# An output projection by Strassen's scheme in a routed-attention and gated-FFN kernel

## The chip, the cores and the metric

One core of one Trainium2 chip runs the whole kernel. The metric is device time of one execution in microseconds (us); smaller is better. The engines are TensorE (PE; PEld is its weight load), VectorE (DVE), ScalarE (ACT), GpSimd (POOL) and SyncE (SP, which here only issues DMAs).

## The reference

Batch 4, 8 heads, 768 tokens, head dimension 64, 16 clusters; then an FFN of 512 to 1536 to 512 over 3072 tokens:

```python
q_assign = argmax(einsum('bhsd,hcd->bhsc', q_n, c_n)); k_assign likewise
scores = where(q_assign == k_assign, scale * q @ k.T, -1e9)
attn = softmax(scores)
x = (attn @ v).transpose(0, 2, 1, 3).reshape(B * S, H * D)
gate = 1 / (1 + exp(-(x @ w_gate)))
out = (gate * (x @ w_val)) @ w_out
```

## The kernel before

The program is written out in full, with the order of each engine fixed by hand: a step is one score matmul, and side work hangs on step numbers in the table `SCHED` (`at`, `plan`, `run_bg`). There are 384 steps, 96 for each batch.

**Attention.** A step (`do_scores`) multiplies a key chunk of 128 with 384 queries into a PSUM bank (`sc`, L655), and ScalarE takes the exponential into `es` (L660). Two steps later (`do_av`) three matmuls of 65 columns add to `av` (L678); the 65th column of V's tile `va` is a constant and gives the denominator. After a head, `normalise` (L342 to L347) divides, on VectorE and GpSimd, and a DMA transposes the result into `xT`. Heads of later batches are made ready in the background (`pair_prep`): raw loads on SP, an fp16 high part (VectorE, L1217) and low part (GpSimd, L1218), a DMA transpose into `T` (`turn`, L382), cluster logits (`lg`, L406), the choice of the cluster (L421 to L441), its one-hot rows moved into `T` by SP (`hop`, L462), and `v_cast` and `v_sum` for V (L294, L302 to L309).

**FFN.** Each batch has two blocks of 384 tokens. For each of 12 chunks of the FFN dimension, `gate` runs four matmuls of 384 columns (`g`, L480) and ScalarE a tanh (L488); `val` runs four more (`v`, L500), and VectorE writes `hT = (tanh + 1) * v` in fp16 (L507). Then `outp` multiplies each of the block's three tiles of 128 tokens with `wo`: 12 matmuls of 512 columns into bank `o` (L520), an eviction that scales by 0.5, on ScalarE (L529) or VectorE (L527), and a store on SP (L532). The very last tile is done in three widths (`closing`, L552 to L562). These pieces, with a cost in ns each, wait in `queue`; after each step `ffn_run(ns)` takes pieces until the budget `ns` of that step is used up. So the FFN of one batch runs between the score matmuls of the next, and the blocks of the last batch run alone at the end.

**PSUM.** Four banks (`ring`) rotate over `sc`, `g`, `v` and `lg`; two hold `av`; two (`op`) hold `o`, and are lent to transposes and V sums (`turns`).

Of the kernel before, what the change touches and what calls it, by code (L numbers as in the profile page):

```python
# [8 lines left out]
FP = mybir.dt.float32  # L9
# [89 lines left out]
def kernel(  # L99
# [44 lines left out]
    tp = pool("T", 10)  # L144
    tbp = pool("TB", 4)
# [9 lines left out]
    osp = pool("os", 3)  # L155
    smp = pool("sm", 3)
# [6 lines left out]

    def turns(n=768, dt=HP, name="turns"):
        return op.tile([128, n], dt, tag="o", name=name)


    WB = SCHED.get("wb", 0)
    warm = const.tile([128, 128 if WB else 512], HP, name="warm")
# [13 lines left out]
    def raw(side):  # L183
        return rawp.tile([128, 2, NCH, 64], FP, tag=f"{side}raw", name=f"{side}raw", bufs=SCHED.get(f"{side}rb", 4))
# [8 lines left out]
    def load(eng, side, b, p):  # L193
        t = RAW[side, b, p] = raw(side)
        eng.dma_start(out=t, in_=view(side, b, p))
# [6 lines left out]
    def load_chunks(eng, side, p, part):  # L202
        if part == 0:
            RAW[side, 0, p] = raw(side)
        c = slice(Q0, NCH) if part else slice(0, Q0)
        eng.dma_start(out=RAW[side, 0, p][:, :, c], in_=view(side, 0, p)[:, :, c])

    def load_half(eng, side, part):
        if (side, 0, 0) not in RAW:
            RAW[side, 0, 0] = raw(side)  # L210
        c = slice(0, Q0) if side == "q" else slice(KC, NCH) if part else slice(0, KC)
        eng.dma_start(out=RAW[side, 0, 0][:, 0, c], in_=view(side, 0, 0)[:, 0, c])
# [17 lines left out]
    WOP = SCHED.get("wop", 2)  # L230
    WON = NFC // WOP
    wo = [wpool.tile([128, WON, DM], HP, name=f"wo{i}") for i in range(WOP)]
# [15 lines left out]


# [34 lines left out]
    vas = [const.tile([128, 2, NCH, 65], HP, name=f"va{i}") for i in range(6)]  # L284
    for t in vas:
        DVE.memset(t[:, :, :, 64:65], 1.0)
    for t in vss:
        DVE.memset(t[:, :, 64:65], float(NCH))
# [178 lines left out]
    def ffn_atoms(xT, t0, n, b, ch, final=False):  # L467
        hT = htp.tile([128, NFC, 384], HP, name="hT")
        gv, outs = [], []
        OA = SCHED.get(f"oa{b}{t0}", SCHED.get("oa", 4))  # L470
        cost = NDC * max(n, 80) / 2.4 + 3

        def gate(fc, st, part):
            def f():
                need(("w", fc // WQ, 0), *(("x", b, p, t0 // 128 + c) for p in range(NP) for c in range(n // 128)))
                if part == 0:
                    st.append(bank(512, name="g"))
                g = st[0]
                for dc in range(GA * part, GA * part + GA):
                    PE.matmul(  # L480
                        out=g[:, 0:n], lhsT=wg[fc // WQ][:, dc, fc % WQ, :],
                        rhs=xT[:, dc, t0 : t0 + n],
                        start=(dc == 0), stop=(dc == NDC - 1),
                    )
                if part < NDC // GA - 1:
                    return
# [6 lines left out]
        def val(fc, st, part):  # L493
            def f():
                need(("w", fc // WQ, 1))
                if part == 0:
                    st.append(bank(512, name="v"))
                w = st[2]
                for dc in range(GA * part, GA * part + GA):
                    PE.matmul(  # L500
                        out=w[:, 0:n], lhsT=wv[fc // WQ][:, dc, fc % WQ, :],
                        rhs=xT[:, dc, t0 : t0 + n],
                        start=(dc == 0), stop=(dc == NDC - 1),
                    )
                if part < NDC // GA - 1:
                    return
                DVE.scalar_tensor_tensor(  # L507
                    hT[:, fc, 0:n], st[1][:, 0:n], 1.0, w[:, 0:n], ALU.add, ALU.mult
                )

            return f

        def outp(t, part, st):
            def f():
                if part == 0:
                    need(*(("wo", i) for i in range(WOP)))
                    st.append(op.tile([128, DM], FP, tag="o", name="o"))
                o = st[0]
                for fc in range(OA * part, OA * part + OA):
                    PE.matmul(  # L520
                        out=o, lhsT=hT[:, fc, bass.ts(t, 128)], rhs=wo[fc // WON][:, fc % WON, :],
                        start=(fc == 0), stop=(fc == NFC - 1),
                    )
                if part == NFC // OA - 1:
                    ob = osp.tile([128, DM], FP, name="ob")
                    if t % 2 or SCHED.get(f"ob{b}{t0}", 0):
                        DVE.tensor_scalar(ob, o, 0.5, None, ALU.mult)  # L527
                    else:
                        ACT.activation(ob, o, AF.Copy, scale=0.5)  # L529

                    def store(ob=ob):
                        SP.dma_start(  # L532
                            out=out[b * S : (b + 1) * S].rearrange("(p c) m -> p c m", c=NCH)[
                                :, ch[t], :
                            ],
                            in_=ob,
                        )

                    d_ = SCHED.get("sd", 0)
                    if d_ > 0 and b < B - 2:  # L540
                        at(step_no[0] + d_, store)
                    else:
                        store()

            return f

        def closing(t, a, z):
            def f():
                w = z - a
                o = bank(w, name="o_end")  # L550
                for fc in range(NFC):
                    PE.matmul(  # L552
                        out=o, lhsT=hT[:, fc, bass.ts(t, 128)],
                        rhs=wo[fc // WON][:, fc % WON, a:z],
                        start=(fc == 0), stop=(fc == NFC - 1),
                    )
                ob = osp.tile([128, w], FP, tag="ob_end", name="ob_end")
                if a:
                    DVE.tensor_scalar(ob, o, 0.5, None, ALU.mult)
                else:  # L560
                    ACT.activation(ob, o, AF.Copy, scale=0.5)
                SP.dma_start(  # L562
                    out=out[b * S : (b + 1) * S].rearrange("(p c) m -> p c m", c=NCH)[
                        :, ch[t], a:z
                    ],
                    in_=ob,
                )

            return f

        for fc in range(NFC):
            st = []
            for i in range(NDC // GA):
                gv.append((cost * GA / NDC, gate(fc, st, i)))
            for i in range(NDC // GA):
                gv.append((cost * GA / NDC, val(fc, st, i)))
        for t in range(n // 128):
            st = []
            if final and t == n // 128 - 1:
                outs.append([(900, closing(t, a, z)) for a, z in SCHED.get("cl", [(0, 256), (256, 384), (384, 512)])])  # L580
            else:
                outs.append([(OA * 216, outp(t, i, st)) for i in range(NFC // OA)])
        return gv, outs

    queue = []
    GA = SCHED.get("ga", 4)

    def ffn_block(*a):
        gv, outs = ffn_atoms(*a)
        for x in gv:  # L590
            queue.append(x)
        for o in outs:
            queue.extend(o)

    def ffn_two(a, b_):
        gv, outs = ffn_atoms(*a)
        gv2, outs2 = ffn_atoms(*b_)
        seq = gv + gv2[0:2]
        for i, o in enumerate(outs):
            seq += o + gv2[2 + 2 * i : 4 + 2 * i]  # L600
        seq += gv2[2 + 2 * len(outs) :]
        for o in outs2:
            seq += o
        queue.extend(seq)

    credit = [0.0]

    def ffn_run(ns):
# [5 lines left out]
        if not queue:  # L614
# [465 lines left out]
    for x in SCHED.get("lo", ["v0", "k1", "q1", "v1", "k2", "q2", "v2", "k3", "q3", "v3"]):  # L1080
        if x == "v0" and SCHED.get("v0h", 0):
            RAW["v", 0, 0] = raw("v")
# [124 lines left out]
    for i in range(WOP):  # L1207
        plan(f"wo{i}", 44 + 6 * i, lambda i=i: load_wo(i))

# [78 lines left out]
    for b in range(B):  # L1288
        xT = xtp.tile([128, NDC, S], HP, tag="xTb", name="xTb")
        key = min(b, 1)  # L1290
        for i in range(2 if b else NPT):
# [5 lines left out]
            for w in range(1 + (cn > 3)):  # L1297
                z = cn // (1 + (cn > 3))
                at(u + lag, lambda xT=xT, b=b, a=c0 + z * w, n=z: ffn_block(
                    xT, 128 * a, 128 * n, b, list(range(a, a + n))))  # L1300
# [18 lines left out]
    ffn_run(1e9)  # L1319
    ffn_block(xT, 384, 384, B - 1, [3, 4, 5], True)  # L1320
# [31 lines left out]
```

## Time and profile before

| | |
|---|---|
| time, median of 3 runs | 326.62 us (326.57 to 326.64) |
| span of the profiled execution, first to last instruction | 326.4 us; its own time is not given apart from the span |
| matmuls of 384 columns: scores, gate, value | 384 each |
| matmuls of 512 columns, output projection | 276, and 36 narrower ones for the last tile |
| scores begin, batch by batch | 8.4, 73.1, 129.7, 206.2 us |
| last score matmul, last matmul | 275.0, 323.0 us |

The span is what the engines' records cover. In the slices a digit is the busy share of an engine in a fortieth of the span, in tenths. In a group's row the first number behind the bar is the busy time of all its instructions in us, the second the mean duration of one in ns.

### The profile page before, as it was taken

The numbers are of one execution on the slowest core, as the hardware profiler recorded it, in microseconds if no ns is written. First come the engines' busy times: TensorE is split into PE (matmuls) and PEld (weight loads), VectorE is DVE, ScalarE is ACT, GpSimd is POOL, SyncE is SP. The second block draws the span as 40 slices with busy tenths as digits, with TensorE's granted clock in tenths as the row PEclk, the third lists the DMA queues.
The fourth block names the chain that finished last, engine by engine and source line by source line (L and its number), as shares of the span: only waits on it lengthen the run. The fifth ranks groups of instructions, "written<-read, shape, count | busy, mean of one in ns | idle before, by whom it ended". The sixth has DMA issues, their size and how long they took to land.

```text
span 326.4 us, 8811 instructions
## 1 busy us (share of the span) xinstructions
PE 318.0 (97%) x3366; PEld 205.8 (63%) x3366; DVE 187.4 (57%) x509; ACT 235.6 (72%) x526; POOL 108.4 (33%) x145
## 2 busy tenths in 40 slices
PE   7899999999999989999999999999999999999996
PEld 4788666766666656666566655666566655654654
DVE  6899567766767766657546655666544322441431
ACT  6788988788899878877677777887778877332420
POOL 6887554054345353324222343323200111000000
PEclk9999999999999999999999999999999999999999
DMA  7999995848977797964795574932731012102002
GB/s 209 358 259 179 263 177 91 207 104 206 242 138 197 138 205 162 257 190 85 124 255 110 169 101 130 238 70 50 141 90 38 2 24 78 44 2 94 6 0 96
DMA packets 77994, 45.14 MB, mean 138 GB/s; under 512 B 56896, under 2 KB 75008, under 8 KB 77952
## 3 DMA queue, kind: packets, MB, share of 16 engines
q1 hardware_dynamic: 73984, 39.73, 50.7%
q0 software_dynamic: 3680, 4.72, 8.7%
q8 instruction: 26, 0.43, 0.5%
q14 instruction: 16, 0.13, 0.1%
q10 hardware_dynamic: 288, 0.13, 0.1%
HBM read 28.34 MB, written 6.29 MB: 106 GB/s over the span
## 4 chain that ended last, share of the span: by engine, by line
PE 86%; DMA 4%; POOL 3%; DVE 3%; issue 2%; SPq 1%; ACT 0%; POOLq 0%
PE g L480 19%; PE v L500 19%; PE o L520 17%; PE sc L655 16%; PE av L678 9%; DMA T<-hl 2%; PE lg L406 2%; DMA kraw<-in_k_dram 2%; PE o_end L552 1%; POOL xp L360 1%; POOL hl L883 1%; POOL hl L1004 1%; PE t_ps L904 0%; PE lg L393 0%; PE t_ps L787 0%
## 5 line engine op out<-in xcount | busy, mean ns | idle before, releaser
L660 ACT ACTIVATE es<-sc 128x384 f16<-128x384 f32 x384 | 175.6, 492 | 42.6 <-PE sc L655 35.6
L655 PE MATMUL sc<-T 128*128 128x384 f16 x384 | 118.0, 325 | 0.7 <-DVE T L985 0.4
L678 PEld LDWEIGHTS <-es 128*128 128x128 f16 x1152 | 81.6, 98 | 49.1 <-ACT es L660 0.2
L678 PE MATMUL av<-va,es 128*128 128x65 f16 x1152 | 97.6, 194 | 0.0
L507 DVE SCALAR_TENSOR_TENSOR hT<-th,v 128x384 f16<-128x384 f32 x96 | 53.1, 554 | 70.3 <-PE av L678 47.4
L500 PE MATMUL v<-xTb,wv 128*128 128x384 f16 x384 | 78.1, 326 | 0.0
L480 PE MATMUL g<-xTb,wg 128*128 128x384 f16 x384 | 78.0, 326 | 0.0
L520 PE MATMUL o<-wo,hT 128*128 128x512 f16 x276 | 75.1, 379 | 0.0
L488 ACT ACTIVATE th<-g 128x384 f32<-128x384 f32 x96 | 47.2, 491 | 25.7 <-DVE hT L507 17.9
L347 POOL TENSOR_TENSOR xp<-t,rec 128x384 f16<-128x384 f32 (+1 forms) x30 | 21.2, 705 | 107.8 <-DVE rec L344 56.4
L480 PEld LDWEIGHTS <-wg 128*128 128x128 f16 x384 | 37.2, 97 | 20.4
L500 PEld LDWEIGHTS <-wv 128*128 128x128 f16 x384 | 37.4, 98 | 19.9
L655 PEld LDWEIGHTS <-T 128*128 128x128 f16 x384 | 37.1, 97 | 1.2 <-DVE T L985 0.7
L520 PEld LDWEIGHTS <-hT 128*128 128x128 f16 x276 | 26.7, 97 | 16.2
L1218 POOL TENSOR_TENSOR hl<-kraw,hl 128x384 f16<-128x384 f32 x22 | 20.4, 925 | 37.5 <-DVE hl L1217 18.2
L342 DVE TENSOR_TENSOR t<-av,sv 128x390 f32<-128x390 f32 (+1 forms) x30 | 14.4, 480 | 20.5 <-PE av L678 16.2
L1218 POOL TENSOR_TENSOR hl<-qraw,hl 128x384 f16<-128x384 f32 x22 | 21.4, 973 | 10.6 <-DVE hl L1217 10.6
L421 DVE TENSOR_REDUCE lgs<-lg 128x192 f32<-128x384 f32 x23 | 12.7, 554 | 13.6 <-PE lg L406 13.6
L529 ACT ACTIVATE ob<-o 128x512 f32<-128x512 f32 x15 | 8.9, 596 | 10.7 <-PE o L520 10.5
L294 POOL CAST va<-vraw 128x768 f16<-128x768 f32 x16 | 13.7, 857 | 2.1 <-DMA vraw<-in_v_dram 2.1
L527 DVE TENSOR_SCALAR ob<-o 128x512 f32<-128x512 f32 x8 | 5.5, 692 | 13.4 <-PE o L520 13.4
L406 PE MATMUL lg<-cm,T 128*128 128x32 f16 x288 | 11.1, 176 | 1.3 <-DMA T<-hl 1.3
(118 smaller groups left out, 239.2 us busy)
## 6 DMA issues: line engine op xcount, KB each, us to landing
vraw<-in_v_dram SPq DMA_DIRECT2D x16, 384.0 KB, 5.9
out_dram<-ob SPq DMA_DIRECT2D x23, 256.0 KB, 2.3
kraw<-in_k_dram SPq DMA_DIRECT2D x15, 384.0 KB, 4.1
qraw<-in_q_dram SPq DMA_DIRECT2D x12, 384.0 KB, 5.0
wg<-in_moe_w_gate_dram POOLq DMA_DIRECT2D x2, 768.0 KB, 9.5
wv<-in_moe_w_val_dram POOLq DMA_DIRECT2D x2, 768.0 KB, 10.5
wo<-in_moe_w_out_dram POOLq DMA_DIRECT2D x2, 768.0 KB, 8.8
qraw<-in_q_dram SPq DMA_DIRECT2D x7, 192.0 KB, 6.9
```

The source lines that it names most:

```text
L342: DVE.tensor_tensor(t[:, 0:nq, :], av, sv, ALU.add)
L347: (eng or POOL).tensor_tensor(x, t[:, 0:nq, 0:64], bcast(rec[:, 0:nq], 64), ALU.mult)
L406: PE.matmul(out=lg[:, bass.ts(i, 32)], lhsT=t[:, c, :], rhs=cm[:, h].rearrange("p s n -> p (s n)"), start=True, stop=True,)
L480: PE.matmul(out=g[:, 0:n], lhsT=wg[fc // WQ][:, dc, fc % WQ, :], rhs=xT[:, dc, t0 : t0 + n], start=(dc == 0), stop=(dc == NDC - 1),)
L488: ACT.activation(th[:, 0:n], g[:, 0:n], AF.Tanh, scale=0.5)
L500: PE.matmul(out=w[:, 0:n], lhsT=wv[fc // WQ][:, dc, fc % WQ, :], rhs=xT[:, dc, t0 : t0 + n], start=(dc == 0), stop=(dc == NDC - 1),)
L507: DVE.scalar_tensor_tensor(hT[:, fc, 0:n], st[1][:, 0:n], 1.0, w[:, 0:n], ALU.add, ALU.mult)
L520: PE.matmul(out=o, lhsT=hT[:, fc, bass.ts(t, 128)], rhs=wo[fc // WON][:, fc % WON, :], start=(fc == 0), stop=(fc == NFC - 1),)
L655: PE.matmul(out=sc.rearrange("p (c t) -> p c t", t=128), lhsT=s["k"], rhs=s["q"], start=True, stop=True,)
L660: ACT.activation(es, sc, AF.Exp, scale=SCALE)
L678: PE.matmul(out=av[:, a0 + s["c0"] + i, :], lhsT=s["es"][:, bass.ts(i, 128)], rhs=VA[b, p][:, e, s["j"], :], start=(first and i == 0 and a ...
L1218: POOL.tensor_tensor(hl[:, :, 64:128], r, hl[:, :, 0:64], ALU.subtract)
```

## The change

For batches b = 1 to 3 the output projection of two tiles of 128 tokens at once is done with seven products instead of eight (the variant of Strassen's scheme with few additions). The FFN dimension is halved (6 chunks each) and so is the output width (256 each). A pair of tiles t1 and t2 plays the two block rows of the left matrix; `wo` and four differences of its parts play the right one. The work falls into these parts:

- *Sums of activations* (`Sums.make`): four fp16 operations of 128x768 per pair on VectorE, put behind given chunks of `val` (`SUMS_AT`); the fourth one behind the product that last reads its input.
- *Differences of weights* (`mix_wo`): four, in two parts each, once, at steps 150 to 204. Three lie in the raw buffers of batch 0's last pair of heads (now `held`), one over a part of `wo`.
- *Products* (`product_out`): seven per group, each of 6 matmuls of 256 columns per pair, alternating between banks x and y; an addition on VectorE (a copy on ScalarE for the first) reads the bank after each product, and two products are added to what the bank already holds.
- *Order*: tiles (0, 1) run as a single pair after block 0, from the list `aside`, every second piece being one of block 1's gate and value pieces. Tiles (3, 2) and (4, 5) run after block 1 as two pairs side by side, in the halves of each bank. While a group is open, `turns` takes a bank of the ring.
- *The factor 0.5* moves into the denominator's constant (2 instead of 1), so the evictions no longer scale, and tanh takes its input as it is.
- *Buffers*: raw tiles 3 per side instead of 4, `T` 8 instead of 10, `va` 5 instead of 6; `wo`'s first row replaces the warm-up tile; output tiles are twice as wide; six `sum` tiles.
- *Budgets* per step for batches 2 and 3 go down by some 4%. The last tile's three widths are gone.

```diff
-    "ns21": 510, "ns22": 500, "ns23": 510, "ns30": 460, "ns31": 460, "ns32": 460, "ns33": 440,
+    "ns21": 491, "ns22": 481, "ns23": 491, "ns30": 443, "ns31": 443, "ns32": 443, "ns33": 423,
-    tp = pool("T", 10)
+    tp = pool("T", 8)
+    sump = pool("sum", 6)
     def turns(n=768, dt=HP, name="turns"):
+        if taken["pair"]:
+            return bank(n, dt, name)
+    def raw(side, b, p):
+        if b == 0 and p == NP - 1:
+            return held[side]
+        return rawp.tile([128, 2, NCH, 64], FP, tag=f"{side}raw", name=f"{side}raw", bufs=3)
+    def mix_wo(i, c):
+        o, a, z = [(T1, B12, B11), (T3, B22, B12), (T2, B22, T1), (T4, B21, T2)][i]
+        c = slice(3 * c, 3 * c + 3)
+        DVE.tensor_tensor(o[:, c], a[:, c], z[:, c], ALU.subtract)
-        DVE.memset(t[:, :, :, 64:65], 1.0)
+        DVE.memset(t[:, :, :, 64:65], 2.0)
-                ACT.activation(th[:, 0:n], g[:, 0:n], AF.Tanh, scale=0.5)
+                ACT.activation(th[:, 0:n], g[:, 0:n], AF.Tanh)
+                for k, x in SUMS_AT[b >= PB, blk].get(fc, []):
+                    sm[x].make(k)
+                if fc == NFC - 1 and pairs and blk == 0:
+                    aside.extend(product_out(b, [sm[(0, 1)]], False))
+    SUMS_AT = {
+        (True, 0): {5: [(3, (0, 1))], 11: [(1, (0, 1)), (2, (0, 1))]},
+        (True, 1): {1: [(1, (3, 2))], 5: [(2, (3, 2)), (3, (3, 2))], 6: [(3, (4, 5))],
+                    11: [(1, (4, 5)), (2, (4, 5))]},
+    }
+        def end1(): ACT.activation(st[C11], st["x"], AF.Copy)
+        def end4(): plus(st[C21], st["y"], st[C11])
+        def end6(): plus(st[C12], st["x"], st[C11])
+        def end5():
+            plus(st[C22], st["y"], st[C11])
+            for m in sums: m.make(4)
+        def end7():
+            plus(st[C21], st["x"], st[C21])
+            plus(st[C22], st["x"], st[C22])
+            for i, m in enumerate(sums): store(st["o2"][:, i], b, m.t2, 1)
+        def end3(): plus(st[C12], st["y"], st[C12])   # stored here at the very end
+        def end2(): plus(st[C11], st["x"], st[C11])   # and stored
+        steps = [
+            ("x", lambda m: tok(b, m.t1, 0), B11, True, end1),
+            ("y", lambda m: tok(b, m.t2, 1), T4, True, end4),
+            ("x", lambda m: m.of[2], T2, True, end6),
+            ("y", lambda m: m.of[1], T1, True, end5),
+            ("x", lambda m: m.of[3], T3, False, end7),
+            ("y", lambda m: m.of[4], B22, False, end3),
+            ("x", lambda m: tok(b, m.t1, 1), B21, True, end2),
+        ]
-        while queue and credit[0] > 0:
-            c, f = queue.pop(0)
+        while (queue or aside) and credit[0] > 0:
+            turn_[0] = 0 if not aside else turn_[0] + 1
+            c, f = (aside if aside and (turn_[0] % 2 == 0 or not queue) else queue).pop(0)
+            plan(f"wt{i}{c}", (150 + 8 * i if i < 3 else 200) + 4 * c, lambda i=i, c=c: mix_wo(i, c))
-    ffn_run(1e9)
-    ffn_block(xT, 384, 384, B - 1, [3, 4, 5], True)
+    ffn_block(xT, 384, 384, B - 1, True)
     ffn_run(1e9)
```

More of the change, by code (lines that the diff above doesn't have):

```diff
@@ L162, in bank, with out_bank @@
         return ring.tile([128, n], dt, tag="ring", name=name)
+    taken = {"op": 0, "pair": False, "last": 1}
+    def out_bank():
+        taken["op"] += 1
+        return op.tile([128, DM], FP, tag="o", name="o")
     def turns(n=768, dt=HP, name="turns"):
+        if taken["pair"]:
+            return bank(n, dt, name)
+        taken["op"] += 1
         return op.tile([128, n], dt, tag="o", name=name)
-    WB = SCHED.get("wb", 0)
-    warm = const.tile([128, 128 if WB else 512], HP, name="warm")
+    WOP = SCHED.get("wop", 2)
+    WON = NFC // WOP
+    wo = [wpool.tile([128, WON, DM], HP, name=f"wo{i}") for i in range(WOP)]
+    WB = 0
+    warm = wo[0][:, 0, :]
     POOL.memset(warm, 0.0)
@@ L464, in hop, with tok, store, f @@
         )
[L467 to L470, printed above, removed]
+    HB = {}
+    def tok(b, t, f):
+        return HB[b, t // 3][:, HF * f : HF * f + HF, bass.ts(t % 3, 128)]
+    def store(src, b, c0, n, m=slice(0, DM)):
+        def f():
+            SP.dma_start(
+                out=out[b * S : (b + 1) * S].rearrange("(p c) m -> p c m", c=NCH)[
+                    :, c0 : c0 + n, m
+                ],
+                in_=src,
+            )
+        d_ = SCHED.get("sd", 0)
+        if d_ > 0 and b < B - 2:
+            at(step_no[0] + d_, f)
+        else:
+            f()
+    def ffn_atoms(xT, t0, n, b, final=False):
+        blk = t0 // 384
+        gv = []
         cost = NDC * max(n, 80) / 2.4 + 3
-        def gate(fc, st, part):
+        pairs = [] if b < PB else [(0, 1)] if blk == 0 else [(3, 2), (4, 5)]
+        sm = {x: Sums(b, *x) for x in pairs}
+        def gate(fc, st):
             def f():
                 need(("w", fc // WQ, 0), *(("x", b, p, t0 // 128 + c) for p in range(NP) for c in range(n // 128)))
[L476 to L479, printed above, removed]
+                if fc == 0:
+                    HB[b, blk] = htp.tile([128, NFC, 384], HP, name="hT")
+                g = bank(512, name="g")
+                for dc in range(NDC):
                     PE.matmul(
@@ L539, in f @@
[L539 to L543, printed above, removed]
-            return f
-        def closing(t, a, z):
-            def f():
-                w = z - a
-                o = bank(w, name="o_end")
-                for fc in range(NFC):
+                    ob = osp.tile([128, 2, DM], FP, name="ob")[:, 0]
+                    if t % 2:
+                        DVE.tensor_copy(ob, o)
+                    else:
+                        ACT.activation(ob, o, AF.Copy)
@@ L583, in ffn_atoms @@
-        return gv, outs
+                        out=st[z][:, e], lhsT=a[:, c, :], rhs=rhs[:, c, :],
+                        start=start and c + e == 0, stop=c == HF - 1, skip_group_check=True,
+                    )
+                if g + G == HF and e == P_ - 1:
+                    end()
+            return f
+        for k in range(7):
+            for e in range(P_):
+                for g in range(0, HF, G):
+                    atoms.append((G * (HD / 2.4 + 2.5), atom(k, e, g)))
+        return atoms
@@ L585 @@
     queue = []
-    GA = SCHED.get("ga", 4)
+    aside = []
     def ffn_block(*a):
[L589 to L604, printed above, removed]
+        queue.extend(ffn_atoms(*a))
```

187 lines of the change are left out of this document (122 added, 65 removed), and 2 rows, old and new, of the table SCHED.

## The prediction

> **What bounds the kernel now.** I read the page first: the share of each engine, the slices, the chain that ended last. Batches are numbered as in the code, b = 0 to 3.
>
> ```profile
> span 326.4 us, 8811 instructions
> PE 318.0 (97%) x3366; PEld 205.8 (63%) x3366; DVE 187.4 (57%) x509; ACT 235.6 (72%) x526; POOL 108.4 (33%) x145
> PE   7899999999999989999999999999999999999996
> DVE  6899567766767766657546655666544322441431
> PEclk9999999999999999999999999999999999999999
> PE 86%; DMA 4%; POOL 3%; DVE 3%; issue 2%; SPq 1%; ACT 0%; POOLq 0%
> ```
>
> The chain is TensorE for 86% of the span, and TensorE is busy in nearly every slice at the full granted clock. Busy time can hide small gaps, so I next took the waits of TensorE alone, and the windows of ten us (columns: length; busy us of PE, PEld, DVE, ACT, POOL with counts; clock; DMA share; GB/s):
>
> ```profile
> PE lg L406 <- DMA T<-hl: 1.3, 1, 1.3
> ...
> 110.00:120.00 10.00, 10.00 (x114) 6.31 (x113) 7.47 (x19) 8.88 (x21) 6.09 (x7) 1.00 0.83 180
> 220.00:230.00 10.00, 10.00 (x103) 6.40 (x102) 7.14 (x18) 7.61 (x18) 4.58 (x5) 1.00 0.33 64
> ```
>
> After the lead-in, one wait stands out: 1.3 us for a transposed tile, near 121 us. Otherwise TensorE never stops, even where VectorE is 71 to 75% busy. So a matmul taken away is worth its full spacing, and a stall put in costs its full length.
>
> **What the change takes from TensorE.** Consecutive matmuls overlap, so the price is not the duration of one but the spacing within a row of the timeline:
>
> ```profile
> 315.26 5.34 PE L520 MATMUL o<-wo,hT 128*128 128x512 f16 x24
> 320.44 1.47 PE L552 MATMUL o_end<-wo,hT 128*128 128x256 f16 x12
> L520 PE MATMUL o<-wo,hT 128*128 128x512 f16 x276 | 75.1, 379 | 0.0
> L552 PE MATMUL o_end<-wo,hT 128*128 128x256 f16 x12 | 1.5, 272 | 0.0
> ```
>
> 512 columns: (5.34 - 0.379) / 23 = 0.2157 us. 256 columns: (1.47 - 0.272) / 11 = 0.1089 us. For b = 1 to 3 there are nine pairs of tiles. A pair took 2 x 12 matmuls of 512 columns; it now takes 7 products x 6 matmuls of 256. 216 x 0.2157 = 46.59 us becomes 378 x 0.1089 = 41.16 us: **-5.43 us**. (The last tile is cut into narrower pieces before; that is under 0.1 us.) The new budgets per step only move matmuls between steps of a full engine, and I cost them at nothing; the cover is the unbroken PE row.
>
> The rows of 256 columns had their 128-column weight loads hidden: twelve loads fit in 1.47 us. The Trainium skill speaks against the change here: "TensorE: Matmul & The Clock Gate", section "Back-to-back issue gap", gives a sustained spacing with weight loads of about 81 ns at 128 columns and 131 ns at 512; a straight line puts 256 at 98 ns, and 378 x 98 - 216 x 131 ns would be an estimated 8.7 us lost. The trace disagrees, with 216 and 109 ns.
>
> **What it adds to VectorE.** Per pair four sums of 128x768 fp16 (36 in all), eight differences of weight parts of the same size (steps 150 to 204), and seven additions per product group from PSUM in place of the 0.5 scalings: 21 of 256 and 21 of 512 elements. Rows for prices (by line, shapes kept apart):
>
> ```profile
> L342 DVE TENSOR_TENSOR t<-av,sv 128x195 f32<-128x195 f32 x12 | 4.3, 359 | 14.3 <-PE av L678 10.6 <-issue 2.0 <-POOL hl L1218 1.7
> L342 DVE TENSOR_TENSOR t<-av,sv 128x390 f32<-128x390 f32 x18 | 10.1, 561 | 6.2 <-PE av L678 5.6 <-POOL hl L1218 0.6
> L917 DVE COPY T<-t_ps 128x768 f16<-128x768 f16 x6 | 3.3, 550 | 0.0
> L883 DVE TENSOR_TENSOR hl<-kraw,hl 128x192 f16<-128x192 f32 x1 | 0.4, 358 | 0.0
> L883 DVE TENSOR_TENSOR hl<-kraw,hl 128x384 f16<-128x384 f32 x1 | 0.5, 548 | 0.0
> L527 DVE TENSOR_SCALAR ob<-o 128x512 f32<-128x512 f32 x8 | 5.5, 692 | 13.4 <-PE o L520 13.4
> L529 ACT ACTIVATE ob<-o 128x512 f32<-128x512 f32 x15 | 8.9, 596 | 10.7 <-PE o L520 10.5
> ```
>
> The L342 rows rise 0.202 us in 195 elements: 0.42 us for 256 elements, 0.69 for 512. No row shows an fp16 sum. Nearest below is the 768-element fp16 copy, 0.55; above, the fp32 pair of L883 carried on to 768, 0.55 + 2 x 0.19 = 0.93. I take 0.55, the same size and type. The Trainium skill ("VectorE: DVE Perf Modes", "What auto-detection actually checks") lets a two-source 16-bit operation reach two elements a cycle, an estimated 0.4 us and a fixed part; no run here shows it yet. Added: 44 x 0.55 + 21 x 0.42 + 21 x 0.69 = 47.5 us, less six scalings of 0.69 and two of 0.29 (4.8): some 43 us. VectorE would be about 70% busy, the level of the two windows above, at which TensorE did not wait. What counts is where single operations stand in front of something.
>
> *The four-bank ring.* Scores, gates and values rotate through four banks:
>
> ```profile
> 253.17 0.81 PE L500 MATMUL v<-xTb,wv 128*128 128x384 f16 x4
> 253.91 0.33 PE L655 MATMUL sc<-T 128*128 128x384 f16 x1
> 254.07 0.81 PE L480 MATMUL g<-xTb,wg 128*128 128x384 f16 x4
> 254.82 0.33 PE L655 MATMUL sc<-T 128*128 128x384 f16 x1
> 254.98 0.81 PE L500 MATMUL v<-xTb,wv 128*128 128x384 f16 x4
> 254.09 0.55 DVE L507 SCALAR_TENSOR_TENSOR hT<-th,v 128x384 f16<-128x384 f32 x1 [0.81 <-PE av L678]
> ```
>
> The bank of the first v is free at 254.64 and wanted by the fourth tile after it at 254.98: 0.34 us of room, and VectorE idle for 0.81 before hT. An operation put ahead of hT is free up to about 1.15 us. Behind a waiting PE stand the next scores, hence the exponentials. In the built order, three places per batch hold two sums, or an addition and a sum, among the logits' operations and v_sum: after chunk 11 of block 0, after chunk 5 of block 1, and behind the fourth product. At 0.55 each, two make 1.1: just hidden. But two SBUF inputs beside GpSimd cost more:
>
> ```profile
> 228.07 1.16 POOL L1218 TENSOR_TENSOR hl<-qraw,hl 128x384 f16<-128x384 f32 x1 [0.86 <-DVE hl L1217]
> 228.50 0.89 DVE L308 TENSOR_TENSOR va<-va 128x128 f32<-128x128 f32 x1
> 248.38 0.28 DVE L308 TENSOR_TENSOR va<-va 128x128 f32<-128x128 f32 x1
> ```
>
> The same operation took 0.89 and 0.28 us. I allow **0.5 us** for both batches (0 to 2.4: six places at 0.4).
>
> *The two product banks, two pairs.* A product is 12 x 0.109 = 1.31 us, and each bank is read before its next product. Inside attention a product spans about 2.1 us with the scores between, and VectorE keeps up, except in b = 1 (whose groups run in b = 2's attention), where the logits' operations stand just before the fourth product's addition; the sixth product then waits some 0.3 us for its sum (0 to 0.8): **0.3**.
>
> In the tail nothing stands between products. From the end of the fourth: signal and addition to 0.8 us, two sums to 1.35 and 1.85 (back to back each adds about 0.5), while the fifth ends at 1.31. The sixth starts 0.1 late. The fifth's bank is read twice, 1.85 to 3.1, and the seventh product, due at 2.7, waits for that: 0.4. Together **0.55 us** (0.3 to 1.35, the upper end with 0.93 per sum).
>
> **The end.**
>
> ```profile
> 323.30 0.29 DVE L559 TENSOR_SCALAR ob_end<-o_end 128x128 f32<-128x128 f32 x1 [0.38 <-PE o_end L552]
> out_dram<-ob SPq DMA_DIRECT2D x23, 256.0 KB, 2.3
> out_dram<-ob_end SPq DMA_DIRECT2D x1, 128.0 KB, 1.7
> out_dram<-ob_end SPq DMA_DIRECT2D x2, 64.0 KB, 1.5
> ```
>
> The last eviction is now 512 elements, 0.69 for 0.29: **+0.4**. The last store is 256 KB instead of 64: 2.3 for 1.5 us to land: **+0.8**. Three more stores of 256 KB are issued in the 2.5 us before it. From 128 to 256 KB the row grows 0.6 us, so four need up to 2.4 us of transfer and the last may queue: **+0.4** (0 to 1.3).
>
> **What is moved on SP.** Three raw buffers per side instead of four (the last pair of batch 0 has its own, in which the weight parts later lie) make loads wait for earlier readers. I compared each load with the last read three pairs back. One is tight:
>
> ```profile
> 112.48 0.83 DVE L1217 CAST hl<-qraw 128x384 f16<-128x384 f32 x1
> 113.03 0.96 POOL L294 CAST va<-vraw 128x768 f16<-128x768 f32 x1
> 113.95 0.91 POOL L1218 TENSOR_TENSOR hl<-qraw,hl 128x384 f16<-128x384 f32 x1
> 113.16 0.47 SPq L195 DMA_DIRECT2D vraw<-in_v_dram  x1
> 114.88 2.46 SPq L382 DMA_TRANSPOSE T<-hl  x1
> 114.88 7.14 DMA T<-hl
> ```
>
> The load of 113.16 now waits for the cast that ends at 113.99. Behind it on SP stand this transpose, the one-hot transpose and the xT transpose. The transpose waits until 114.86 for GpSimd anyway, so that costs nothing. Two weight differences fall before the cast of 112.48, 1.1 us together (1.9 at most), against 0.64 between the cast's end and GpSimd's start and the quarter of this window in which VectorE is idle. The transpose may start 0 to 1.2 us later, and its landing ends the 1.3 us wait found above: **+0.2**. T with 8 buffers and va with 5 are freed many steps before reuse.
>
> **Sum.** -5.43 + 0.5 + 0.3 + 0.55 + 0.4 + 0.8 + 0.4 + 0.2 = -2.28. The profiled span is 326.4; the median of three runs, 326.62, lies 0.2 above it, and I keep that: 326.62 - 2.28 = **324.3 us**.
>
> **Rivals.**
> *Only the columns and the last store count*: all new VectorE work hides, no stall but the last 0.3 of the tail, stores not queued. -5.43 + 0.3 + 0.4 + 0.8 = -3.9, 322.7 us. For it: 43% of VectorE is idle. Against: the bank is read twice before the seventh product.
> *The tail takes it*: sums at 0.93 in the tail (1.35) and the stores fully queued (1.3), the rest as forecast: -5.43 + 1.0 + 1.35 + 1.2 + 1.3 = -0.6, about 326.0.
> *VectorE becomes the bound in attention*: sums at 0.93 and held by GpSimd for 0.6. Two make 2.5 us before an hT against the cover of 1.15 and one product part between (3 x 0.109): about 1.0 us of TensorE at each of six places. 6.0 + 0.8 + 0.2 + 1.35 + 1.6 - 5.43 = +4.5, 331 us; it decides from 0.5 us a place. For it: 0.89 us at 228.50. Against: GpSimd is busy 46% even from 220 to 230 us, so not every sum meets it.
> *Weight loads set the spacing*, so that each of 162 extra matmuls costs a load:
>
> ```profile
> L520 PEld LDWEIGHTS <-hT 128*128 128x128 f16 x276 | 26.7, 97 | 16.2
> ```
>
> 162 x 0.097 = 15.7 on top: about 340 us; the 109 ns spacing speaks against it. The section of the Trainium skill named above is the rule behind it.
>
> **How the numbers follow.** About 0.2%, 0.65 us, is what a measurement can tell from no change. Forecast 0.58 (322.4 to 325.9); only columns 0.10; tail 0.10, of which 0.06 within 0.2%; VectorE bound 0.19; weight loads 0.03. Faster 0.72, same 0.06, slower 0.22. The range runs from the columns alone to the near part of the VectorE case, 322.4 to 327.0, and leaves out the rest of that case and the weight loads.
>
> **What would show it.** Right: 378 matmuls 109 ns apart in the o rows; no wait of PE on hT above a few tenths; a wait of about 0.4 before the last product; 1.6 us more between last matmul and end. Wrong: sums of 0.9 us or more, waits of PE for hT or sum adding up to over 3 us, a spacing above 123 ns (24 x 0.2157 / 42, where the product scheme stops paying), or a longer wait of lg near 121 us.

## The result, and the profile after

| | before | after |
|---|---|---|
| time, median of 4 runs each, same chip | 326.60 us (326.33 to 326.64) | 324.82 us (324.73 to 324.90) |
| ratio to before, 95% interval | | 0.9944 [0.9930, 0.9958] |
| profiled execution: time, span | 326.62, 324.8 us (profile taken again, e1_before) | 324.90, 323.1 us |

The change makes the kernel 1.8 us faster; the forecast was 2.3 us. The kernel before was run and profiled once more beside the experiments. That second profile is the one to compare with: its lines and the page of after are next.

The page of the kernel before, profiled again, its timeline of the cluster logits near 121 us, and its end (columns: start us, us, engine, line, operation):

```profile
span 324.8 us, 8811 instructions
120.50 0.46 PE L406 MATMUL lg<-cm,T 128*128 128x32 f16 x12
318.87 2.81 PE L552 MATMUL o_end<-wo,hT 128*128 128x256 f16 x36
321.72 0.29 DVE L559 TENSOR_SCALAR ob_end<-o_end 128x128 f32<-128x128 f32 x1 [0.38 <-PE o_end L552]
```

The page of the kernel after:

```profile
span 323.1 us, 9150 instructions
PE 314.7 (97%) x3504; PEld 222.1 (69%) x3504; DVE 226.7 (70%) x586; ACT 231.1 (72%) x520; POOL 108.6 (34%) x145
PE   7999999999999999999999999999999999999994
DVE  6899656777667997576879688576867356555654
PEclk9999999999999999999999999999999999999999
PE 87%; DVE 5%; issue 3%; DMA 2%; POOL 1%; SPq 0%; ACT 0%; POOLq 0%; DVEq 0%
```

TensorE still carries the chain. VectorE has 39 us more work and is 70% busy. The row near 120.5 us has no wait in its brackets: the 1.3 us wait for a transposed tile, which the first profile showed, is not there when the same kernel is profiled again.

The waits of TensorE alone, kernel after, from 40 us on (total us, times, longest), and windows of ten us (busy us of PE, PEld, DVE, ACT, POOL; clock; DMA share; GB/s):

```profile
PE sc L788 <- DVE lgs L449: 0.6, 1, 0.6
PE g L529 <- DMA xTb<-xp: 0.5, 1, 0.5
PE o L716 <- DVE sum L632: 0.2, 1, 0.2
PE o L716 <- DVE ob L658: 0.2, 1, 0.2
...
110.00:120.00 10.00, 9.43 (x105) 5.91 (x104) 9.65 (x23) 8.34 (x20) 6.11 (x7) 1.00 0.74 201
190.00:200.00 10.00, 9.79 (x122) 8.11 (x120) 8.17 (x21) 6.16 (x13) 3.14 (x5) 1.00 0.34 74
220.00:230.00 10.00, 10.00 (x110) 6.76 (x108) 8.11 (x21) 7.99 (x19) 3.43 (x4) 1.00 0.51 100
```

The view has four waits, each of them once, and TensorE loses time in the windows in which they lie. At 81% VectorE (220 to 230 us) it loses none; at 97% (110 to 120 us) it loses half a us.

The groups of the kernel after, shapes kept apart (busy us, mean ns of one, idle before):

```profile
L716 PE MATMUL o<-wo,hT 128*128 128x256 f16 x162 | 24.0, 272 | 0.2 <-DVE ob L658 0.2
L626 DVE TENSOR_TENSOR sum<-hT 128x768 f16<-128x768 f16 x9 | 5.9, 650 | 0.2
L632 DVE TENSOR_TENSOR sum<-hT,sum 128x768 f16<-128x768 f16 x9 | 4.7, 550 | 0.0
L276 DVE TENSOR_TENSOR vheld<-wo,wo 128x768 f16<-128x768 f16 x2 | 1.6, 798 | 0.0
L658 DVE TENSOR_TENSOR ob<-o,ob 128x512 f32<-128x512 f32 x21 | 14.1, 688 | 9.6 <-PE o L716 8.9 <-ACT es L793 0.7
L658 DVE TENSOR_TENSOR ob<-o,ob 128x256 f32<-128x256 f32 x21 | 8.4, 414 | 0.1
```

The prices taken for the sums (0.55) and for the additions (0.42 and 0.69) are met where nothing disturbs them. The first sums (650) and the first weight differences (798 here) come out longer.

**Where the 1.71 us of span come from**, from the starts of matmuls, the profile before taken again against the one after. The columns give -5.46, by the count of matmuls and their full-rate spacing. Time lost by spacing is what a matmul starts later than one full-rate spacing behind the one before it; after 40 us it grows from 1.51 to 4.05 us, +2.54. The lead-in before 40 us has +0.32 (it differs by up to 0.7 us among profiles of versions of the kernel after that are alike up to there). From the start of the last matmul to the end of the span it is 4.27 us instead of 3.38, +0.89. The sum is -1.71.

### The profile page after: what moved, and what is told of

The parts are those of the page before. It is cut to its first block, busy times and chain, and to the rows that moved or that the text cites. A ratio compares the mean times of both kernels' runs of the same rounds, so it can differ in the third digit from the quotient of the medians.

```text
span 323.1 us, 9150 instructions
## 1 busy us (share of the span) xinstructions
PE 314.7 (97%) x3504; PEld 222.1 (69%) x3504; DVE 226.7 (70%) x586; ACT 231.1 (72%) x520; POOL 108.6 (34%) x145
## 4 chain that ended last, share of the span: by engine, by line
PE 87%; DVE 5%; issue 3%; DMA 2%; POOL 1%; SPq 0%; ACT 0%; POOLq 0%; DVEq 0%
PE g L529 19%; PE v L545 19%; PE sc L788 17%; PE av L811 10%; PE o L716 10%; PE o L583 4%; PE lg L434 2%; PE oh_ps L1097 1%; PE lg L421 1%; PE t_ps L1037 1%; DMA xTb<-xp 1%; DMA qraw<-in_q_dram 1%; PE wm L879 1%; DVE ob L658 1%; POOL xp L375 1%
## 5 line engine op out<-in xcount | busy, mean ns | idle before, releaser
L658 DVE TENSOR_TENSOR ob<-o,ob 128x256 f32<-128x256 f32 (+1 forms) x42 | 22.6, 551 | 9.7 <-PE o L716 8.9
L716 PEld LDWEIGHTS <-sum 128*128 128x128 f16 x216 | 20.9, 98 | 5.6 <-DVE sum L632 0.7
L716 PE MATMUL o<-wo,hT 128*128 128x256 f16 x162 | 24.0, 272 | 0.2 <-DVE ob L658 0.2
L1354 POOL TENSOR_TENSOR hl<-qraw,hl 128x384 f16<-128x384 f32 x22 | 20.7, 940 | 10.0 <-DVE hl L1353 9.7
L583 PE MATMUL o<-wo,hT 128*128 128x512 f16 x72 | 19.9, 379 | 0.0
L716 PEld LDWEIGHTS <-hT 128*128 128x128 f16 x162 | 15.7, 97 | 4.2 <-issue 0.4
L322 POOL CAST va<-vraw 128x768 f16<-128x768 f32 x15 | 12.9, 860 | 2.5 <-DMA vraw<-in_v_dram 2.5
```

The source lines that it names most:

```text
L583: PE.matmul(out=o, lhsT=HB[b, blk][:, fc, bass.ts(t, 128)], rhs=wo[fc // WON][:, fc % WON, :], start=(fc == 0), stop=(fc == NFC - 1),)
L658: plus = lambda dst, a, z: DVE.tensor_tensor(dst, a, z, ALU.add)
L716: PE.matmul(out=st[z][:, e], lhsT=a[:, c, :], rhs=rhs[:, c, :], start=start and c + e == 0, stop=c == HF - 1, skip_group_check=True,)
L1354: POOL.tensor_tensor(hl[:, :, 64:128], r, hl[:, :, 0:64], ALU.subtract)
```

## The experiments

After the result the theory was: the columns pay as forecast, and what is given back goes to a few single places, where a sum, a weight difference or an addition stands in front of something on VectorE, and to the end. The rivals: the loss is spread out, because VectorE is simply fuller; or part of the gain or loss belongs to the other edits (budgets, buffers, the factor 0.5, the undivided last tile), not to the products. e1 to e4 ran on one chip, e5 to e8 on a second, e9 and e10 on a third, each beside the kernel before (326.80, 326.60 and 326.96 us there).

**e1_before: the kernel before, profiled again.** No edit.

> The kernel before, unchanged, to see how its time stands to its span; the changed kernel's time lies 1.8 us above its span. If that offset is common to both, the span here should be near 324.8 us. If the change itself adds something outside the span, the span here stays at 326.4 us and the time at 326.6.

Measured: 326.66 us (326.26 to 327.15), ratio 0.9997 [0.9986, 1.0008]; its profiled execution took 326.62 us with a span of 324.8, and has no wait of `lg`. So the time lies 1.8 us above the span, as in the kernel after (324.90 to 323.1). The first profile, with its span of 326.4, had caught an execution with a wait that is not typical of the kernel: the ten executions of this run have spans of 324.5 to 325.4 us.

**e2_plain: everything but the products.**

```diff
-    PB = 1
+    PB = 4
-    for i in range(4):
-        for c in range(2):
-            plan(f"wt{i}{c}", (150 + 8 * i if i < 3 else 200) + 4 * c, lambda i=i, c=c: mix_wo(i, c))
```

> The changed kernel with the seven products switched off: batches 1 to 3 use the twelve matmuls of 512 columns as batch 0 does, and no weight differences are made; buffers, budgets, the constant 2 and the undivided last tile stay. My theory (TensorE's spacing pays, the other edits cost nothing): span within 0.5 us of the kernel before, time 326.3 to 327.2. Rival (the smaller buffers or budgets give or take time by themselves): over 1 us away. If the 1.5 us outside the span come from these other edits, they show here too.

Measured: 327.54 us (327.16 to 327.83), ratio 1.0021 [1.0011, 1.0031], span 325.6. The other edits together cost 0.9 us, more than the theory allowed and less than the rival asked; the products are worth 2.7 us on top of them (327.54 to 324.82). Of the cost, 0.56 us is the undivided last tile (3.94 us from last matmul start to end, 3.38 before). Two gates lose 0.31 us each; the first, in the timeline of e2:

```profile
186.64 0.19 DVE L372 RECIPROCAL rec<-t 128x6 f32<-128x6 f32 x1
186.85 0.55 DVE L550 SCALAR_TENSOR_TENSOR hT<-th,v 128x384 f16<-128x384 f32 x1
187.46 0.81 PE L529 MATMUL g<-xTb,wg 128*128 128x384 f16 x4
```

The gate's bank is freed by an `hT` that stands behind a head's division. No sum is near: a place in the ring is lost here by the order of the steps alone. Which of the other edits moved it was not taken apart.

**e3_mixlate: the weight differences from step 193 on.** In the kernel after, the first ones lie near 113 us (DVE, POOL and PE in the timeline of after):

```profile
113.12 1.07 DVE L276 TENSOR_TENSOR vheld<-wo,wo 128x768 f16<-128x768 f16 x1
114.11 0.97 DVE L1353 CAST hl<-qraw 128x384 f16<-128x384 f32 x1
115.01 0.54 DVE L449 TENSOR_REDUCE lgs<-lg 128x192 f32<-128x384 f32 x1
112.86 0.91 POOL L1354 TENSOR_TENSOR hl<-kraw,hl 128x384 f16<-128x384 f32 x1 [0.35 <-POOL xp L375]
115.61 0.32 PE L788 MATMUL sc<-T 128*128 128x384 f16 x1 [0.57 <-DVE lgs L449]
```

The difference starts while GpSimd's operation of 112.86 runs, and ends 0.4 us after that one's end at 113.77: it takes 1.07 us instead of the 0.55 that the same shape takes when undisturbed. The Trainium skill ("SBUF — State Buffer", "Who interferes with whom") states that a VectorE instruction with two SBUF inputs is blocked by a GpSimd instruction that reads SBUF and was issued first, until that one is finished; the trace agrees. The cast and the reading of the logits' bank follow it on VectorE, and the next scores want that bank: 0.74 us of TensorE, counted by spacing.

```diff
-            plan(f"wt{i}{c}", (150 + 8 * i if i < 3 else 200) + 4 * c, lambda i=i, c=c: mix_wo(i, c))
+            plan(f"wt{i}{c}", 193 + 7 * i + 3.5 * c, lambda i=i, c=c: mix_wo(i, c))
```

> The eight weight differences are moved from steps 150 to 204 to steps 193 to 218, all else as in the changed kernel. My theory: the wait of 0.7 us of a score matmul on the logits near 115 us goes, and the wait of 1.5 us for the transposed tile near 122 us, which the kernel before has and the changed one lacks, comes back in part, because the order on SP moves back: between -0.7 and +0.8 us. Rival (the differences merely load VectorE): about 0.7 us faster.

Measured: 323.51 us (323.32 to 325.19), ratio 0.9913 [0.9885, 0.9940], span 321.8. The 0.74 us is gone; the wait for `xTb` falls from 0.62 to 0.11; spacing losses after 40 us fall from 4.05 to 3.10. Another 0.40 us is a shorter lead-in, which the edit does not touch. So the span is 1.4 us shorter, more than theory and rival had, and not all of it is the edit's. The wait for `xTb` changes from execution to execution: e6 and e8, the same program up to there, have 0.22 and 0.44. One of the four executions took 325.19 us, so the interval meets that of the kernel after. A wait near 121 us did not come back.

**e4_sum6: the fourth sum behind another addition.** The sums made in `end5` stand in front of the sixth product (0.38 us by spacing in attention, 0.10 in the tail).

```diff
+        def end6(): plus(st[C12], st["x"], st[C11])
+            for m in sums: m.make(4)
         def end5():
             plus(st[C22], st["y"], st[C11])
-            for m in sums: m.make(4)
```

> The fourth sum of each pair is made one product earlier, behind the addition of the third product instead of the fourth. My theory: the waits before the sixth and seventh products of two pairs side by side go (0.38 us near 196 us, 0.10 and 0.34 us near 316 us): 0.5 to 0.9 us faster than the changed kernel. Rival (VectorE as a whole is too loaded, so the wait only moves): within 0.3 us of it.

Measured: 324.65 us (324.54 to 324.82), ratio 0.9936 [0.9922, 0.9951], 0.17 us from the kernel after. The timeline of e4 (DVE, PE):

```profile
195.47 1.88 DVE L658 TENSOR_TENSOR ob<-o,ob 128x512 f32<-128x512 f32 x3
196.20 0.49 PE L716 MATMUL o<-wo,sum 128*128 128x256 f16 x3 [0.62 <-DVE ob L658]
```

In attention the wait changed its name and grew, from 0.38 on the sum to 0.78 on the additions queued behind the logits' operations. In the tail, with no logits, the two waits of 0.10 and 0.34 became one of 0.23. The rival, that the wait only moves, holds in attention; the theory holds in the tail.

**e5_budget: e3 with the budgets of before.**

```diff
-    "ns20": 500, "ns21": 491, "ns22": 481, "ns23": 491, "ns30": 443, "ns31": 443, "ns32": 443, "ns33": 423,
+    "ns20": 520, "ns21": 510, "ns22": 500, "ns23": 510, "ns30": 460, "ns31": 460, "ns32": 460, "ns33": 440,
```

> On the kernel with the later weight differences: the budgets per step of batches 2 and 3 back at the values of the kernel before. In the kernel without products two gates waited 0.31 us each for a bank whose VectorE reader stood behind a head's division. My theory (the lower budgets moved the values onto the divisions; what is left is worth a few tenths): 0.3 us faster to 0.3 us slower. Rival (the lower budgets are needed because the products are shorter): over 0.5 us slower.

Measured: 326.50 us (324.42 to 327.23), ratio 0.9975 [0.9953, 0.9997], span 324.7: nearly the whole gain is gone, as the rival had it. The timeline of e5 (PE, SP), and windows of one us with the columns above:

```profile
196.36 0.25 PE L811 MATMUL av<-va,es 128*128 128x65 f16 x3
198.98 1.64 SPq L842 DMA_TRANSPOSE xTb<-xp  x1
202.30 0.32 PE L529 MATMUL g<-xTb,wg 128*128 128x384 f16 x1 [1.99 <-DMA xTb<-xp]
204.29 1.49 PE L529 MATMUL g<-xTb,wg 128*128 128x384 f16 x4
...
201.00:202.00 1.00, 0.00 (x0) 0.00 (x0) 0.81 (x3) 0.00 (x0) 0.34 (x1) 1.00 0.34 131
203.00:204.00 1.00, 1.00 (x8) 0.49 (x6) 0.00 (x0) 0.53 (x2) 0.00 (x0) 0.50 0.90 203
205.00:206.00 1.00, 1.00 (x7) 0.55 (x6) 0.00 (x0) 0.27 (x2) 0.91 (x1) 0.50 1.28 285
```

The first gate of batch 2's FFN comes up at 199.7 us, almost as in e3 (199.8). What moves is its data. The old budgets work the queue off sooner, so the last steps of attention are done later: the `av` matmuls from whose division this tile is made end at 196.6 us instead of 195.7, and the transpose is issued 1.2 us later than in e3. TensorE waits 2.0 us, and then the granted clock is 0.50 for about 3.4 us (the five windows from 202 to 207 us have 0.95, 0.50, 0.50, 0.50 and 0.85): four gate matmuls take 1.49 us instead of 0.81. So the wait costs more than its own length. Not every execution has the lower clock: in six of the ten, the profiled one among them, the mean granted clock is 0.992 to 0.995, and they took 326.47 to 327.23 us; the four at 1.000 took 324.42 to 325.88 us, still 0.9 us or more above the median of e3.

**e6_split: e3 with the last addition and store cut in two.**

```diff
-            plus(st[C11], st["x"], st[C11])
-                store(st[C11], b, sums[0].t1, P_, slice(0, HD))
+                for i in range(P_):
+                    plus(st[C11][:, i], st["x"][:, i], st[C11][:, i])
+                    store(st[C11][:, i : i + 1], b, sums[0].t1 + i, 1, slice(0, HD))
```

> On the kernel with the later weight differences: the very last addition of 512 elements and its store of 256 KB are cut into two of 256 elements and 128 KB, one for each tile. My theory, from the rows (0.69 becomes twice 0.42, landing 2.3 becomes 1.7 us): the last landing comes 0.3 to 0.5 us earlier. Rival (the four last stores queue for the same transfer, so nothing is won): within 0.15 us.

Measured: 323.50 us (323.25 to 323.66), ratio 0.9895 [0.9870, 0.9919], against 323.51 and 0.9913 for e3. The trace has 4.08 us from the last matmul start to the end, 4.25 in e3: 0.17 us, about half of the least that was forecast and too little to show in the times.

**e7_double: e3 with the first three sums of each pair of b = 1 and 2 written twice.** The 18 added operations change no value.

```diff
+            for _ in range(2 if self.b < B - 1 and i < 4 else 1):
                 if i == 1:
                     DVE.tensor_tensor(o, a2(0), a2(1), ALU.add)
```

> On the kernel with the later weight differences: in batches 1 and 2 the first three sums of each pair are written twice, 18 more operations of VectorE, some 10 us of its time. My theory (VectorE has room except where an operation stands right before something due): 0.3 to 1.5 us slower. Rival (VectorE is the bound in attention): about 5 us slower or more.

Measured: 326.75 us (326.15 to 327.29), ratio 0.9996 [0.9981, 1.0012], span 324.9. Ten us more on VectorE (18 at 0.55 to 0.65) cost 3.2 us. The dearest place is one (timeline of e7, DVE and PE):

```profile
260.25 1.30 DVE L627 TENSOR_TENSOR sum<-hT 128x768 f16<-128x768 f16 x2
261.57 1.15 DVE L629 TENSOR_TENSOR sum<-sum,hT 128x768 f16<-128x768 f16 x2
262.64 0.29 DVE L346 TENSOR_SCALAR sv<-vs_ps 128x130 f32<-128x130 f32 x1
262.98 0.49 PE L719 MATMUL o<-wo,hT 128*128 128x256 f16 x3 [1.05 <-DVE sv L346]
```

Four sums in a row hold up the operation that empties a borrowed product bank, and the next product waits 1.2 us by spacing. Two of them there, as in the kernel after, cost nothing. So VectorE has some room but little: one operation more at each place, and a third of the added time comes through. Both the theory (single places) and the rival (spread out) had wrong sizes here.

**e8_lastplain: e3 with the last batch by plain matmuls of 512 columns.**

```diff
+    plain = lambda b: b < PB or b == B - 1
-        if b < PB:
+        if plain(b):
```

> On the kernel with the later weight differences: the last batch by plain matmuls of 512 columns, batches 1 and 2 by products (the fourth weight difference has a tile of its own, output tiles two instead of three). By the spacing 3 pairs lose 1.81 us; the two waits of the tail (0.45) and part of its end (0.3) come back: my theory 0.9 to 1.3 us slower than with products. Rival (in the tail the products' additions eat the gain): as fast or faster.

Measured: 324.88 us (324.22 to 325.15), ratio 0.9934 [0.9908, 0.9961]. The two intervals overlap, so the traces are compared: span 323.2 against 321.8. The columns cost +1.81 us (by count and spacing, a third of 5.43), the `xTb` wait, which varies by execution, +0.33; the tail's two waits give back 0.45 and the end 0.17. These come to 1.5, where the spans differ by 1.4. On the same chip e6, with products in all three batches, took 323.25 to 323.66 us, every execution below the fastest of e8. So the products pay in the last batch as well, stalls and end included.

**e9_late23: e3, the fourth sum moved in the tail alone, and a lower budget in the last stage of batch 2.**

```diff
-    "ns23": 491,
+    "ns23": 471,
+            if final:                  # in end6; in end5 only if not final
+                for m in sums: m.make(4)
```

> On the kernel with the later weight differences: the fourth sums a product earlier in the very last group alone, where no other VectorE work stands between, and the budget of the last quarter of batch 2's steps 20 ns lower. My theory: in the tail the waits of 0.10 and 0.34 us shrink by 0.2 (as they did with all sums earlier), and the gates of the next block reach the transposed x later, so that this wait (0.1 to 0.6 us, run by run) goes: 0.2 to 0.7 us faster. Rival (other values now meet a head's division): within 0.2 us.

Measured: 323.72 us (322.79 to 323.92), ratio 0.9891 [0.9861, 0.9921]. The forecast gain did not come, and the rival is nearer. The tail's waits went from 0.45 to 0.23, but the wait for `xTb` rose from 0.11 to 0.82: the `av` matmuls that its division needs end 0.6 us earlier than in e3, but the division still stands behind two additions of a product and starts only 0.15 us earlier; the transpose takes 3.1 us from issue to landing instead of 2.5, and the gate comes up 0.3 us earlier.

**e10_all2: e3 with that tail, and all four budgets of batch 2 lower.**

```diff
-    "ns20": 500, "ns21": 491, "ns22": 481, "ns23": 491,
+    "ns20": 490, "ns21": 481, "ns22": 471, "ns23": 481,
```

> The same, but with all four budgets of batch 2 lower by 10 ns, which moves the place of every value in that batch. My theory, that single meetings on VectorE decide: between 0.5 us faster and 0.5 us slower than the kernel with the later weight differences, and not the same waits as in the run before it. Rival (lower is better throughout): faster than the run with one budget lower.

Measured: 323.09 us (322.84 to 323.21), ratio 0.9876 [0.9855, 0.9897], span 321.4. The view of waits has no row for TensorE after 40 us (by spacing 0.25 us are left at `xTb` and 0.23 in the tail), and the spacing losses are down from 4.05 to 2.44 us. This is the best version found, 1.2% faster than before; its interval lies below that of the change as made, but meets those of e3 and e9, so theory and rival are not told apart.

## Why the prediction was right, and where it was not

**Columns: right.** Forecast -5.43, measured -5.46; e8 shows a third of it for one batch. Rows of twelve matmuls of 256 columns take 1.47 us as before, so the weight loads stay hidden, and the rival in which they set the spacing (340 us) falls.

**The price of a sum: right where it was taken.** 0.55 us in the tail and in the L632 row, 0.58 to 0.65 for the others, 0.80 to 0.91 for the first two kinds of weight differences. VectorE grew by 39 us where 43 were forecast (in that sum the scalings that go are 4.7 us, not 4.8). The rival in which it becomes the bound needed 0.5 us at each of six places; no such series is in the trace. Yet e7 shows that rival to be near: one more operation at each place takes away the whole gain.

**The two product banks: right.** In b = 1 the sixth product waits 0.38 us for its sum (forecast 0.3); in the tail it waits 0.10 and the seventh 0.34 (forecast 0.1 and 0.4). The tail in the timeline of after, PE and DVE:

```profile
314.58 1.47 PE L716 MATMUL o<-vheld,sum 128*128 128x256 f16 x12
316.00 1.48 PE L716 MATMUL o<-wo,sum 128*128 128x256 f16 x12
317.66 1.47 PE L716 MATMUL o<-wo,hT 128*128 128x256 f16 x12 [0.18 <-DVE ob L658]
314.79 0.69 DVE L658 TENSOR_TENSOR ob<-o,ob 128x512 f32<-128x512 f32 x1 [0.62 <-PE o L716]
315.39 1.02 DVE L632 TENSOR_TENSOR sum<-hT,sum 128x768 f16<-128x768 f16 x2
316.33 1.89 DVE L658 TENSOR_TENSOR ob<-o,ob 128x512 f32<-128x512 f32 x3
319.17 0.69 DVE L658 TENSOR_TENSOR ob<-o,ob 128x512 f32<-128x512 f32 x1 [0.96 <-PE o L716]
```

It is the order forecast: addition, two sums, then the fifth bank's two additions ahead of the seventh product. The three additions of 316.33 are the two of `end7` and the one of `end3`.

**The end: one part mis-sized, one wrong.** The last eviction takes 0.69 for 0.29 (+0.40, as forecast). The last store lands 2.08 us after its issue, the one of before 1.52: +0.56 for a forecast of 0.8. It did not queue behind the three before it (forecast +0.4): these were issued at 317.64, 318.02 and 318.54 and had landed by 320.96; it was issued at 319.89 and landed at 321.97, sooner than the 2.3 us taken for such a store alone. In all +0.89 where 1.6 was forecast. The times of issue were foreseen (within 2.5 us before the last). The error was the allowance for queueing: at the prediction's own price of 0.6 us of transfer a store, the three stores issued 1.35 to 2.25 us ahead are nearly done when the last one comes.

**SP and the weight differences: the right chain, the wrong victim.** The prediction had the two differences delay the cast near 112.5 us, with GpSimd's contention as the upper end (1.9 us), and read the cost off the transpose: +0.2 on the 1.3 us wait near 121. That wait was a feature of the one execution profiled, and the slip of the transpose (114.88 to 116.11) cost nothing. The cost came in the same queue of VectorE: the bank of the logits is read behind the delayed cast, and the scores wait 0.74 us for that bank. e3 shows it.

**The ring: right in size, wrong in place.** Forecast 0.5 us for sums ahead of an `hT`. The trace has 0.31 and 0.13 us of gates waiting, but e2, without any sum, has 0.31 twice.

**Budgets at nothing, under "the unbroken PE row": this step failed.** The budgets decide how much of attention is still to be done when the side work is, and so how much time the last head's result has to reach the first gate of the FFN: from `av` (PE) to the division (VectorE), the product (GpSimd), the transpose (SP) and the gate (PE). First the kernel after, then the kernel before, profiled again:

```profile
196.25 0.25 PE L811 MATMUL av<-va,es 128*128 128x65 f16 x3
196.24 1.28 DVE L658 TENSOR_TENSOR ob<-o,ob 128x512 f32<-128x512 f32 x2
197.44 0.35 DVE L370 TENSOR_TENSOR t<-av,sv 128x195 f32<-128x195 f32 x1
198.08 0.54 POOL L375 TENSOR_TENSOR xp<-t,rec 128x192 f16<-128x192 f32 x1 [4.21 <-DVE rec L372]
198.65 1.86 SPq L842 DMA_TRANSPOSE xTb<-xp  x1
201.72 0.32 PE L529 MATMUL g<-xTb,wg 128*128 128x384 f16 x1 [0.46 <-DMA xTb<-xp]
...
196.47 0.26 PE L678 MATMUL av<-va,es 128*128 128x65 f16 x3
198.47 1.21 SPq L709 DMA_TRANSPOSE xTb<-xp  x1
```

The table has the room, from the end of these `av` matmuls to the moment at which the gate's fourth matmul, the one that waits, would come up at full rate, and what uses it (us, from the traces):

| | room | `av` to issue of the transpose | issue to landing | left |
|---|---|---|---|---|
| before again (e1): old budgets, no products | 4.90 | 1.75 | 2.30 | +0.84 |
| e2: lower budgets, no products | 6.70 | 1.33 | 2.32 | +3.05 |
| after: lower budgets, products | 4.60 | 2.15 | 3.03 | -0.58 |
| e3: the same, differences later | 4.60 | 2.15 | 2.53 | -0.07 |
| e5: old budgets, products | 3.53 | 2.37 | 3.28 | -2.12 |
| e10: still lower budgets in batch 2, products | 5.58 | 1.76 | 4.03 | -0.21 |

The products take room away and the lower budgets give it back. In the kernel after, TensorE loses 0.62 us by spacing here. From +0.84 before to -0.58 it is 1.42 us: 0.39 because two additions of a product hold the division up (it starts 0.94 us behind its `av`, before 0.55 behind an eviction), 0.30 of room, and 0.73 of slower landing. Why this transpose lands later in the kernels with products stays open. The prediction asked what stands before an `hT`, and not what stands before a division, nor how much time its result has. With the old budgets the wait is 2.0 us and the clock falls (e5 against e3, 3.0 us in the median): the lower budgets, costed at nothing, are what keeps most of the gain. That they were in the change was no part of the forecast's reasoning, so here the forecast had luck.

**The offset: wrong, and in part cancelled.** The prediction set the median 0.2 us above the span of 326.4. In both kernels the time lies 1.8 us above the span; the first profile was of an execution some 1.6 us longer than the kernel's usual one. The change in time, -1.78, is the one to hold against the -2.28 of the sum. Too high in the sum were the end (1.6 for 0.89) and the transpose (0.2 for 0); too low were the two unforeseen waits (0.74 and 0.62) and the lead-in (0.32). That the sum came within half a us of the measured change is in part such cancelling.

## What to carry to other kernels

Where the bounding engine has no gaps, a scheme that saves its columns pays at the measured spacing, and what is given back lies at a few single places. Look for them by asking, of each operation added to another engine's queue, which bank or tile the next operations behind it set free: not only the obvious one (`hT`), but casts, logits and divisions too. When work on the bounding engine shrinks, retune what paces the side work: at the old pace the side work was done early here, the last steps of attention were done late, and their result had too little time to reach its reader. Profile the kernel before twice, ahead of building on a wait that one execution shows.

## What the runs showed of the hardware that was not expected

One idle stretch of 2.0 us on TensorE (e5) was followed by a granted clock of 0.50 for about 3.4 us. The Trainium skill ("TensorE: Matmul & The Clock Gate", section "What's actually happening") puts that fall behind an idle window of about 3.4 us; here 2.0 us were enough, in a stretch of 4 us (199 to 203) of which TensorE was busy for 2.0. How long the wait was in the other executions of e5, five with the lower mean clock and four without, is not known. The waits of 0.6 and 0.5 us in the kernel after, and of 1.2 us in e7, left the clock at 1.00.
